# Chaining the last block's division and projection into the issue order of an attention + GLU kernel, with retuned scheduler constants and a VectorE-only prologue scaling

## Chip, cores, metric

The kernel runs on 1 core of a Trainium2 chip. The metric is the device time of one execution in microseconds (us); lower is better. Three runs of the kernel before gave a median of 854.28 us.

Engine names as in the profile: PE (TensorE, matmuls), PEld (its weight loads), DVE (VectorE), ACT (ScalarE), POOL (GpSimd), SP (SyncE, which issues most DMAs). PV is the product of probabilities and values. In the views a q behind a name (SPq) means that engine's sequencer, which waits and issues; "issue" is time in which the profile shows no wait. The granted clock (PEclk) is the share of its full clock that TensorE is given: 1.00 is full, 0.50 half. In code cuts `...` marks what is left out, and comments behind # are partly added here.

## The reference

Sequence 2048, width 640, 32 heads of 20, GLU width 1728, bf16:

```python
xn = layernorm(x)
s  = softmax(q k^T * 20**-0.5) v @ wo          # q, k, v = xn @ wqkv, 32 heads
g  = silu((sigmoid(xn @ w_gate) * (xn @ w_up)) @ w_down)
return x + s * g
```

## The kernel before

The kernel has three stages. In the *prologue* the rows of x (16 tiles of 128) are normalised, scaled, transposed, and the first keys and queries are made. In the *middle* 32 blocks of attention (8 groups of 4 heads, 4 query chunks of 512) run with the GLU woven in. In the *tail* comes what is left of the output projection, and the last block.

The instruction order of the middle is made when the program is built: a small Python loop keeps a model time for PE, ScalarE and VectorE and decides at each step what an engine gets next. Its decisions depend on a line of tuning constants:

```python
URGENT, ROUNDS, HOLD, SLACK, LEAD, LAG, D_LAST, D_LAST_END = 0.05, 3, 0.2, 0.6, 40.0, 0.0, 24, 16
D_ORD, M_ORD, WAIT3, FALL, M_END = 0, 1, 0.0, 1, 1.5
```

The result is a static order: each engine works its list from front to back, and a late item holds up all behind it.

Exponentials are shared. ScalarE does most of the 2048 score tiles with its exp, two per instruction (1024 columns), sometimes with a third of 512 columns. VectorE does the others by integer arithmetic (`iv`, then three passes over four tiles).

The prologue's scaling, some of it on GpSimd:

```python
POOL_XN = (0, 1, 4, 5)
...
(nc.gpsimd if eng == "POOL" else nc.vector).tensor_scalar(
    out=xns[k], in0=xts[k], scalar1=mvs[c][:, i, 0:1], scalar2=rstds[c][:, i, :],
    op0=ALU.subtract, op1=ALU.mult)
```

An output half-tile (128 rows, 320 columns) is an item of the issue order; there are 24 for the first three chunks. Its rows of x and of the gate `gq` come by DMA into one of three slots, and the result is stored from that slot:

```python
o2 = xfl[:, tt % 3 * KD * QC: ...]                         # the slot of row tile tt
nc.sync.dma_start(out=out_tiles[tt][0], in_=x2[...])       # x: waits for the store of row tile tt - 3
nc.sync.dma_start(out=out_tiles[tt][1], in_=gq_dram[...])
...
nc.vector.scalar_tensor_tensor(out=tmp, in0=st["ps"][:, 0:HD], scalar=0.25, in1=gqr[:, sl], ...)
nc.gpsimd.tensor_tensor(out=xr[:, sl], in0=tmp, in1=xr[:, sl], op=ALU.add)   # needs x
```

After the loop `tail_steps()` emitted the last block's division and projection in one go: copy `oacc`, transpose, divide, transpose back, with the early matmuls (those that don't need the last block's result) of four 512-column groups ("mains") in between; then the late matmul of each main (the one that needs it); then a fifth group ("rest", 128 columns of each of four row tiles), then the evictions.

Of the kernel before, what the change touches and what calls it, by code (L numbers as in the profile page):

```python
# [10 lines left out]
FP32 = mybir.dt.float32  # L11
# [7 lines left out]
P = 128  # L19
# [11 lines left out]
URGENT, ROUNDS, HOLD, SLACK, LEAD, LAG, D_LAST, D_LAST_END = 0.05, 3, 0.2, 0.6, 40.0, 0.0, 24, 16  # L31
D_ORD, M_ORD, WAIT3, FALL, M_END = 0, 1, 0.0, 1, 1.5
# [17 lines left out]
def kernel(  # L50
# [146 lines left out]
    ACT_STATS = (3, 6, 7, 11, 14, 15)  # L197
    POOL_XN = (0, 1, 4, 5)
    with tc.tile_pool(name="ln", bufs=2) as lp, \
# [68 lines left out]
        def s_xn(eng, k):  # L268
            c, i = divmod(k, 4)
            xns[k] = lp.tile([P, D], BF16, tag="xn", bufs=TT, name="xn")  # L270
            (nc.gpsimd if eng == "POOL" else nc.vector).tensor_scalar(
                out=xns[k], in0=xts[k], scalar1=mvs[c][:, i, 0:1], scalar2=rstds[c][:, i, :],
                op0=ALU.subtract, op1=ALU.mult)
# [63 lines left out]
        for c in range(NQC):  # L337
            ks = range(4 * c, 4 * c + 4)
            st = [Step(s_stats, (k,), {"ACT": 1.62} if k in ACT_STATS else {"DVE": 0.83},
                       (table,) if k in ACT_STATS else (), 3.2 + 0.5 * k, late=0.5 * c) for k in ks]  # L340
            rs = Step(s_rstd, (c,), {"POOL": 1.3}, st, late=2.0 * c)
            for k in ks:
                xn = Step(s_xn, (k,), {"POOL": 0.85} if k in POOL_XN else {"DVE": 0.40}, (rs,), late=2.0 * c)
                tr = Step(s_tr, (k,), {"PE": 0.6}, (xn, idt), take="tp", late=2.0 * c)
                evs.append(Step(s_ev, (k,), {"DVE": 0.46, "ACT": 0.62}, (tr,), give="tp", late=2.0 * c))
            km = Step(s_k, (c,), {"PE": 1.1}, (spread, *evs[4 * c:]), take="pk", late=2.0 * c)
            kts.append(Step(s_kt, (c,), {"ACT": 0.58}, (km, ones), late=2.0 * c))
            kms.append(Step(s_kmax, (c,), {"DVE": 0.62}, (km, kts[-1]), give="pk", late=2.0 * c))
            for i in range(2 if c < NVP else 0):
                vm = Step(s_v, (c, i), {"PE": 0.9}, evs[4 * c:], take="pv", late=2.0 * c + 5.0)  # L350
                Step(s_vev, (c, i), {"ACT": 0.33}, (vm, consts), give="pv", late=2.0 * c + 5.0)
# [319 lines left out]
    def mk_down(c, t4, h, at):  # L671
# [15 lines left out]
        def ev():  # L687
            gqs = w2.tile([P, HD], FP32, tag="gqs", bufs=2, name="gqs")
# [57 lines left out]
    def mk_out(tt, h, at):  # L746
# [21 lines left out]
        def ev():  # L768
            xr, gqr = out_tiles[tt]
            sl = slice(h * HD, (h + 1) * HD)  # L770
            tmp = w2.tile([P, HD], FP32, tag="gqs", bufs=2, name="otmp")
            nc.vector.scalar_tensor_tensor(out=tmp, in0=st["ps"][:, 0:HD], scalar=0.25,
                                           in1=gqr[:, sl], op0=ALU.mult, op1=ALU.mult)
            nc.gpsimd.tensor_tensor(out=xr[:, sl], in0=tmp, in1=xr[:, sl], op=ALU.add)
# [190 lines left out]

    def tail_steps():
        c0 = (NQC - 1) * QC
        mains = [scA[1][:, 0, :], scA[1][:, 1, :], bank[0], bank[1]]

        def early(dst, t4, sl, stop):  # L970
            for kd in range(t_l + 1):
                rows = P if kd < t_l else o_l
                nc.tensor.matmul(dst, lhsT=oU[0:rows, kd, c0 + t4 * P:c0 + (t4 + 1) * P], rhs=wo[0:rows, kd, sl],
                                 start=(kd == 0), stop=stop and kd == t_l, skip_group_check=True)

        def late_mm(dst, t4, sl):
            nc.tensor.matmul(dst, lhsT=o7[:, t4 * P:(t4 + 1) * P], rhs=wo_l[:, sl], start=False, stop=True,
                             skip_group_check=True)

        on = w2.tile([P, QC], FP32, tag="on", bufs=2, name="on")  # L980
        nc.vector.tensor_copy(out=on, in_=oacc)
        early(mains[0], 0, slice(0, 512), False)
        early(mains[1], 1, slice(0, 512), False)
        tps = scA[0][:, 0, :]
        for i in range(4):
# [367 lines left out]
```

## Time and profile before

The stages, read off the timeline (first score matmul, end of the last PV matmul):

| stage | us | what limits it |
|---|---|---|
| prologue | 0 to 37.2 | a chain over all engines, POOL in it |
| middle | 37.2 to 818.1 (780.9) | ACT, PE and DVE together |
| tail | 818.1 to 849.5 (31.4) | PE, with a stop; ACT idle |

The windows view of before, one line per stage; after the stretch and its length come each engine's busy us with the number of instructions, then the granted TensorE clock, the DMA share and GB/s:

```profile
core 0: us, PE busy (x) PEld busy (x) DVE busy (x) ACT busy (x) POOL busy (x), PEclk, DMA share, GB/s
0.00:37.20 37.20, 16.64 (x146) 11.10 (x149) 22.89 (x58) 23.07 (x50) 23.27 (x36) 1.00 0.46 123
37.20:818.10 780.90, 752.86 (x6108) 253.92 (x6161) 741.84 (x1127) 771.26 (x928) 55.34 (x42) 1.00 0.25 69
818.10:849.50 31.40, 22.44 (x118) 10.25 (x119) 12.15 (x23) 0.00 (x0) 11.56 (x14) 0.83 0.36 113
```

In the middle ACT is busy 771 of 781 us, PE 753, DVE 742. In the tail the mean clock is 0.83. The 1.00 of the prologue is not all true: the clock record begins at 23.1 us only, and before that the five key matmuls of 512 columns took 2.34 us (at 20.84 us, below), the spacing of half clock.

The timeline of before, prologue (start, duration, engine, line, operation, out<-in):

```profile
9.04 5.00 POOL L271 TENSOR_SCALAR xn<-xt,mv,rstd 128x640 bf16<-128x640 bf16 x2
...
14.09 0.72 PE L278 MATMUL tp<-ident,xn 128*128 128x128 bf16 x5 [1.77 <-POOL xn L271]
...
17.60 5.17 POOL L271 TENSOR_SCALAR xn<-xt,mv,rstd 128x640 bf16<-128x640 bf16 x2
...
20.34 0.72 PE L278 MATMUL tp<-ident,xn 128*128 128x128 bf16 x5 [4.02 <-POOL xn L271]
...
20.84 2.34 PE L140 MATMUL psk<-xnT,wqk_85 128*128 128x512 bf16 x5
```

Two scalings on POOL take 5.0 and 5.2 us. The transposes at 14.09 and 20.34 wait for POOL (the bracket names it), and the first key matmul follows the second of these at 20.84.

The chain of waits of before, tail (start, duration, what): each line is what released the next.

```profile
822.74 4.33 DMA xnT<-in_A_x_dram
...
827.20 0.80 POOL xnT L774
...
828.02 0.50 DVE otmp L772
...
828.57 1.93 PE bk_511 L765 x6
830.50 1.83 PE bk_510 L765 x6
...
832.54 3.78 PE scA_508 L973 x9
```

A load of x takes 4.33 us to land. POOL's add waits for it, DVE waits for POOL, and PE for the bank that DVE empties. After that nine matmuls of 512 columns take 3.78 us, 0.42 each. The windows view of before around that stop:

```profile
825.30:828.70 3.40, 1.88 (x11) 0.80 (x10) 0.49 (x1) 0.00 (x0) 1.50 (x2) 0.99 0.77 244
828.70:832.10 3.40, 3.40 (x12) 1.23 (x11) 0.98 (x2) 0.00 (x0) 2.36 (x4) 0.50 0.48 152
832.10:835.50 3.40, 3.18 (x8) 0.99 (x8) 1.09 (x2) 0.00 (x0) 0.79 (x1) 0.50 0.13 49
835.50:839.00 3.50, 3.50 (x21) 1.51 (x18) 1.17 (x3) 0.00 (x0) 0.00 (x0) 1.00 0.00 0
```

From 828.7 to 835.5 the clock is 0.50.

### The profile page before, as it was taken

How to read it: one execution, taken by the hardware profiler on the slowest of the kernel's cores; microseconds unless marked ns; L12 is line 12 of the kernel's file. 1: busy time of each engine (PE TensorE's matmuls, PEld its weight loads, DVE VectorE, ACT ScalarE, POOL GpSimd, SP SyncE). 2: the span in 40 equal slices, each digit the busy share in tenths (PEclk: the TensorE clock that was granted, in tenths of full speed). 3: DMA queues.
4: the chain of work that ended last, by engine and by line, in shares of the span. 5: the costliest groups of instructions: out<-in, count | busy, mean ns of one | idle time of the engine just before them, and what ended most of it. 6: DMA issues, size and time to landing. Idle time of an engine off the chain costs nothing.

```text
span 849.5 us, 16987 instructions
## 1 busy us (share of the span) xinstructions
PE 791.9 (93%) x6369; PEld 275.3 (32%) x6424; DVE 776.9 (91%) x1208; ACT 794.3 (94%) x978; POOL 90.2 (11%) x92
## 2 busy tenths in 40 slices
PE   1899999999999999999999999999999999999996
PEld 1532322333333323333333222333333222233342
DVE  7589999999899998998999999999989989999964
ACT  6799999999999999999999999999999999999940
POOL 7300000000000000000000010000000000001242
PEclk9999999999999999999999999999999999999997
DMA  5531311123221233213122222220411331112551
GB/s 152 149 91 43 79 50 39 51 61 79 65 65 52 59 84 84 65 39 80 41 60 57 67 79 65 73 79 26 124 60 46 84 84 44 29 46 70 184 161 65
DMA packets 92979, 62.21 MB, mean 73 GB/s; under 512 B 34648, under 2 KB 86408, under 8 KB 92896
## 3 DMA queue, kind: packets, MB, share of 16 engines
q1 hardware_dynamic: 92608, 60.79, 25.8%
q8 instruction: 50, 0.82, 0.4%
q14 instruction: 33, 0.27, 0.1%
q10 hardware_dynamic: 288, 0.33, 0.1%
HBM read 46.24 MB, written 12.39 MB: 69 GB/s over the span
## 4 chain that ended last, share of the span: by engine, by line
PE 34%; ACT 28%; DVE 27%; issue 6%; DMA 2%; POOL 2%; SPq 1%; POOLq 0%; DVEq 0%; ACTq 0%
DVE iv L1168 11%; PE oacc L896 7%; PE scA_508 L859 5%; PE scA_507 L859 5%; DVE pb L950 4%; DVE pb L947 3%; PE bk_511 L641 3%; DVE pb L944 3%; PE bk_510 L641 2%; PE bk_509 L641 2%; PE bk_511 L504 1%; PE bk_511 L679 1%; PE bk_510 L679 1%; ACT tnh L80 1%; PE bk_510 L504 1%
## 5 line engine op out<-in xcount | busy, mean ns | idle before, releaser
L950 DVE TENSOR_TENSOR pb<-iv,pb 128x2048 bf16<-128x2048 bf16 x121 | 150.8, 1246 | 0.4
L1168 DVE TENSOR_SCALAR iv<-bk_509 128x512 int16<-128x512 f32 x168 | 114.2, 680 | 8.6 <-PE bk_509 L859 8.5
L1168 DVE TENSOR_SCALAR iv<-bk_510 128x512 int16<-128x512 f32 x168 | 114.4, 681 | 7.1 <-PE bk_510 L859 6.9
L926 POOL TENSOR_TENSOR on_bf<-on,rl 128x512 bf16<-128x512 f32 x30 | 43.2, 1440 | 693.3 <-DMA rl<-rd 342.6
L1168 DVE TENSOR_SCALAR iv<-bk_511 128x512 int16<-128x512 f32 x148 | 101.0, 682 | 9.4 <-PE bk_511 L859 9.0
L944 DVE TENSOR_SCALAR pb<-iv 128x2048 int16<-128x2048 int16 x121 | 88.3, 730 | 2.6
L947 DVE TENSOR_SCALAR pb<-iv 128x2048 int16<-128x2048 int16 x121 | 88.2, 729 | 0.0
L859 PEld LDWEIGHTS <-kT_81 32*128 32x128 bf16 x1024 | 40.4, 91 | 142.1 <-issue 137.7
L859 PEld LDWEIGHTS <-kT_82 32*128 32x128 bf16 x1024 | 44.2, 91 | 122.6 <-issue 112.1
L641 PE MATMUL bk_511<-xnT,wgu 128*128 128x512 bf16 x262 | 75.6, 382 | 2.7 <-DVE iv L1168 0.7
L896 PE MATMUL oacc<-pb,v_84 128*21 128x512 bf16 x498 | 74.1, 382 | 0.4 <-DVE pb L950 0.4
L896 PE MATMUL oacc<-pb,v_83 128*21 128x512 bf16 x470 | 73.3, 382 | 0.9 <-DVE pb L950 0.7
L641 PEld LDWEIGHTS <-wgu 128*128 128x128 bf16 x520 | 39.0, 97 | 68.5 <-issue 47.1
L679 PEld LDWEIGHTS <-hT 128*128 128x128 bf16 x448 | 35.8, 97 | 45.8 <-issue 36.0
L896 PEld LDWEIGHTS <-v_84 128*21 128x21 bf16 x1273 | 26.2, 90 | 47.3 <-issue 36.2
L896 PEld LDWEIGHTS <-v_83 128*21 128x21 bf16 x1259 | 25.9, 90 | 47.2 <-issue 37.5
L641 PE MATMUL bk_510<-xnT,wgu 128*128 128x512 bf16 x125 | 37.4, 382 | 2.1 <-DVE iv L1168 1.1
L679 PE MATMUL bk_509<-wd,hT 128*128 128x320 bf16 (+1 forms) x168 | 32.5, 302 | 0.5 <-DVE gqs L689 0.3
L679 PE MATMUL bk_511<-wd,hT 128*128 128x320 bf16 (+1 forms) x168 | 31.8, 302 | 0.3 <-DVE hT L661 0.2
L859 PE MATMUL scA_507<-q_94,kT_82 32*128 32x512 bf16 x134 | 27.1, 383 | 2.5 <-ACT pt_2836 L80 0.9
L859 PE MATMUL scA_507<-q_93,kT_81 32*128 32x512 bf16 x141 | 27.9, 383 | 1.5 <-DVE q_93 L177 0.8
L859 PE MATMUL scA_508<-q_93,kT_81 32*128 32x512 bf16 x140 | 27.9, 384 | 1.1 <-ACT pt_6542 L80 0.3
(1790 smaller groups left out, 2303.8 us busy)
## 6 DMA issues: line engine op xcount, KB each, us to landing
wgu<-in_B_w_gate_dram SPq DMA_DIRECT2D x24, 320.0 KB
wgu<-in_B_w_up_dram SPq DMA_DIRECT2D x24, 320.0 KB
rl<-rd SPq DMA_DIRECT2D x120, 64.0 KB
gq_dram<-gqs SPq DMA_DIRECT2D x32, 160.0 KB
xnT<-gq_dram SPq DMA_DIRECT2D x12, 320.0 KB
xt<-in_A_x_dram SPq DMA_DIRECT2D x16, 160.0 KB
wd<-in_B_w_down_dram SPq DMA_DIRECT2D x1, 2080.0 KB
oU<-on_bf SPq DMA_DIRECT2D x104, 20.0 KB
```

The costliest lines, as they stand in the source:

```text
L80: return nc.scalar.add_instruction(mybir.InstActivation(func=func, name=nc.get_next_instruction_name(), engine=ENG.Activation, ins=[nc.sca ...
L504: nc.tensor.matmul(st["ps"][0:UC, :], lhsT=wus[u][:, kd, i, :], rhs=xnT[:, c, kd, :], start=(kd == 0), stop=(kd == KD - 1))
L641: nc.tensor.matmul(st[key][0:fs, :], lhsT=w[:, i, kd, ko * P:ko * P + fs], rhs=xnT[:, c, kd, :], start=(kd == 0), stop=(kd == KD - 1))
L679: nc.tensor.matmul(st["ps"][:, 0:HD], lhsT=hT[0:fsz[kf], kf, t4 * P:(t4 + 1) * P], rhs=wd[0:fsz[kf], kf, h * HD:(h + 1) * HD], start=(kf = ...
L859: nc.tensor.matmul(dst, lhsT=kTs[(b // NQC) % 2][32 * j:32 * j + 32, kt * P:(kt + 1) * P], rhs=qts[b % 3][32 * j:32 * j + 32, :], start=Tr ...
L896: nc.tensor.matmul(oacc[32 * j:32 * j + DH + 1, :], lhsT=lhsT, rhs=u["src"], start=first, stop=last, tile_position=(0, 32 * j), skip_group ...
L926: nc.gpsimd.tensor_tensor(out=on_bf, in0=on, in1=rl, op=ALU.mult)
L944: nc.vector.tensor_scalar(out=pb[:, 0, :, :].bitcast(I16), in0=iv, scalar1=0x7F80, scalar2=1, op0=ALU.bitwise_and, op1=ALU.bitwise_or)
L947: nc.vector.tensor_scalar(out=pb[:, 1, :, :].bitcast(I16), in0=iv, scalar1=0x007F, scalar2=0x3F00, op0=ALU.bitwise_and, op1=ALU.bitwise_or)
L950: nc.vector.tensor_tensor(out=pb[:, 1, :, :], in0=iv.bitcast(BF16), in1=pb[:, 1, :, :], op=ALU.mult)
L1168: nc.vector.tensor_scalar(out=d["iv"][:, j, :], in0=bank[bk], scalar1=B_OFF, scalar2=0.0, op0=ALU.add, op1=ALU.max)
```

## The change

Its intent: the last block's division should be issued step by step between the output half-tiles that are left, so that PE and DVE don't wait for each other; the prologue's scalings leave POOL; and the constants are tuned again. The core of the diff:

```diff
-URGENT, ROUNDS, HOLD, SLACK, LEAD, LAG, D_LAST, D_LAST_END = 0.05, 3, 0.2, 0.6, 40.0, 0.0, 24, 16
-D_ORD, M_ORD, WAIT3, FALL, M_END = 0, 1, 0.0, 1, 1.5
+URGENT, ROUNDS, HOLD, SLACK, LEAD, LAG, D_LAST, D_LAST_END = 0.25, 4, 0.15, 0.2, 40.0, 0.0, 20, 8
+D_ORD, M_ORD, WAIT3, FALL, M_END = 1, 0, 0.4, 1, 1.5
...
-    ACT_STATS = (3, 6, 7, 11, 14, 15)
-    POOL_XN = (0, 1, 4, 5)
+    L_ST, L_CH = 6.0, 2.0                 # statistics of later chunks rank behind the chain of earlier ones
+    ACT_STATS = (3, 7, 9, 11, 13, 15)
...
-            (nc.gpsimd if eng == "POOL" else nc.vector).tensor_scalar(
+            nc.vector.tensor_scalar(
...
-            kms.append(Step(s_kmax, (c,), {"DVE": 0.62}, (km, kts[-1]), give="pk", late=2.0 * c))
+            kms.append(Step(s_kmax, (c,), {"DVE": 0.62}, (km,), give="pk", late=L_CH * c))
...
-            tmp = w2.tile([P, HD], FP32, tag="gqs", bufs=2, name="otmp")
+            tmp = w2.tile([P, HD], FP32, tag="gqs", bufs=3, name="otmp")
...
-            nc.gpsimd.tensor_tensor(out=xr[:, sl], in0=tmp, in1=xr[:, sl], op=ALU.add)
+            add = nc.vector if h == 1 and claimed[0] == NJOB * NBLK else nc.gpsimd
+            add.tensor_tensor(out=xr[:, sl], in0=tmp, in1=xr[:, sl], op=ALU.add)
...
+    chain = [("DVE", 0.60, e_on), ("PE", 1.52, e_tr), ("DVE", 0.75, e_scale), ("PE", 0.42, e_back), ("DVE", 0.45, e_o)]
+    fill = [... the early matmuls of the four mains, then of the rest ...]
     def tail_steps():
-        ... (division, early and late matmuls, as told above)
+        for _, _, f in fill:
+            f()
+        for t4 in range(4):
+            late_mm(rest[:, t4 * EX:(t4 + 1) * EX], t4, slice(512, D))
+        for t4 in range(4):
+            late_mm(mains[t4], t4, slice(0, 512))
...
+            if free["PE"] <= now and chain and chain[0][0] == "PE" and chain_at <= now:
+                _, dur, f = chain.pop(0)      # the same for DVE; fill is taken when nothing else is left
```

More of the change, by code (lines that the diff above doesn't have):

```diff
@@ L338 @@
             ks = range(4 * c, 4 * c + 4)
-            st = [Step(s_stats, (k,), {"ACT": 1.62} if k in ACT_STATS else {"DVE": 0.83},
-                       (table,) if k in ACT_STATS else (), 3.2 + 0.5 * k, late=0.5 * c) for k in ks]
-            rs = Step(s_rstd, (c,), {"POOL": 1.3}, st, late=2.0 * c)
+            st = [Step(s_stats, (k,), {"ACT": 1.92} if k in ACT_STATS else {"DVE": 0.98},
+                       (table,) if k in ACT_STATS else (), 3.2 + 0.5 * k, late=L_ST * c) for k in ks]
+            rs = Step(s_rstd, (c,), {"POOL": 1.3}, st, late=L_CH * c)
             for k in ks:
-                xn = Step(s_xn, (k,), {"POOL": 0.85} if k in POOL_XN else {"DVE": 0.40}, (rs,), late=2.0 * c)
-                tr = Step(s_tr, (k,), {"PE": 0.6}, (xn, idt), take="tp", late=2.0 * c)
-                evs.append(Step(s_ev, (k,), {"DVE": 0.46, "ACT": 0.62}, (tr,), give="tp", late=2.0 * c))
-            km = Step(s_k, (c,), {"PE": 1.1}, (spread, *evs[4 * c:]), take="pk", late=2.0 * c)
-            kts.append(Step(s_kt, (c,), {"ACT": 0.58}, (km, ones), late=2.0 * c))
-            kms.append(Step(s_kmax, (c,), {"DVE": 0.62}, (km, kts[-1]), give="pk", late=2.0 * c))
+                xn = Step(s_xn, (k,), {"DVE": 0.42}, (rs,), late=L_CH * c)
+                tr = Step(s_tr, (k,), {"PE": 0.6}, (xn, idt), take="tp", late=L_CH * c)
+                evs.append(Step(s_ev, (k,), {"DVE": 0.46, "ACT": 0.62}, (tr,), give="tp", late=L_CH * c))
+            km = Step(s_k, (c,), {"PE": 1.1}, (spread, *evs[4 * c:]), take="pk", late=L_CH * c)
+            kts.append(Step(s_kt, (c,), {"ACT": 0.58}, (km, ones), late=L_CH * c))
+            kms.append(Step(s_kmax, (c,), {"DVE": 0.62}, (km,), give="pk", late=L_CH * c))
             for i in range(2 if c < NVP else 0):
-                vm = Step(s_v, (c, i), {"PE": 0.9}, evs[4 * c:], take="pv", late=2.0 * c + 5.0)
-                Step(s_vev, (c, i), {"ACT": 0.33}, (vm, consts), give="pv", late=2.0 * c + 5.0)
+                vm = Step(s_v, (c, i), {"PE": 0.9}, evs[4 * c:], take="pv", late=L_CH * c + 5.0)
+                Step(s_vev, (c, i), {"ACT": 0.33}, (vm, consts), give="pv", late=L_CH * c + 5.0)
             if c == 0:
@@ L687, in ev @@
         def ev():
-            gqs = w2.tile([P, HD], FP32, tag="gqs", bufs=2, name="gqs")
+            gqs = w2.tile([P, HD], FP32, tag="gqs", bufs=3, name="gqs")
             nc.vector.scalar_tensor_tensor(out=gqs, in0=st["td"], scalar=1.0, in1=st["ps"][:, 0:HD],
@@ L964, in tail_load @@
             nc.sync.dma_start(out=tail[t4][1], in_=gq_dram[r, :])
-    def tail_steps():
-        c0 = (NQC - 1) * QC
-        mains = [scA[1][:, 0, :], scA[1][:, 1, :], bank[0], bank[1]]
-        def early(dst, t4, sl, stop):
-            for kd in range(t_l + 1):
-                rows = P if kd < t_l else o_l
-                nc.tensor.matmul(dst, lhsT=oU[0:rows, kd, c0 + t4 * P:c0 + (t4 + 1) * P], rhs=wo[0:rows, kd, sl],
-                                 start=(kd == 0), stop=stop and kd == t_l, skip_group_check=True)
-        def late_mm(dst, t4, sl):
-            nc.tensor.matmul(dst, lhsT=o7[:, t4 * P:(t4 + 1) * P], rhs=wo_l[:, sl], start=False, stop=True,
-                             skip_group_check=True)
-        on = w2.tile([P, QC], FP32, tag="on", bufs=2, name="on")
-        nc.vector.tensor_copy(out=on, in_=oacc)
-        early(mains[0], 0, slice(0, 512), False)
-        early(mains[1], 1, slice(0, 512), False)
-        tps = scA[0][:, 0, :]
-        for i in range(4):
-            nc.tensor.transpose(out=tps[:, i * P:(i + 1) * P], in_=on[:, i * P:(i + 1) * P], identity=ident_f)
-        onq = div_scale(tps)
-        early(mains[2], 2, slice(0, 512), False)
-        tp2 = psum.tile([P, 2 * QC], BF16, name="tp2", tag="oacc")
-        for i in range(4):
-            nc.tensor.transpose(out=tp2[0:GC, i * P:(i + 1) * P], in_=onq[:, i, :], identity=ident)
-        early(mains[3], 3, slice(0, 512), False)
-        o7 = w2.tile([GC, QC], BF16, tag="on_bf", bufs=2, name="o7")
-        nc.vector.tensor_copy(out=o7, in_=tp2[0:GC, 0:QC])
@@ new lines, with early, late_mm @@
+    c0 = (NQC - 1) * QC
+    mains = [scA[1][:, 0, :], scA[1][:, 1, :], bank[0], bank[1]]
+    rest = bank[2]
+    last = {}
+    def early(dst, t4, sl, kd, start=True):
+        rows = P if kd < t_l else o_l
+        nc.tensor.matmul(dst, lhsT=oU[0:rows, kd, c0 + t4 * P:c0 + (t4 + 1) * P], rhs=wo[0:rows, kd, sl],
+                         start=(start and kd == 0), stop=False, skip_group_check=True)
+    def late_mm(dst, t4, sl):
+        nc.tensor.matmul(dst, lhsT=last["o"][:, t4 * P:(t4 + 1) * P], rhs=wo_l[:, sl], start=False, stop=True,
+                         skip_group_check=True)
@@ new lines, in e_on, with e_tr, e_scale, e_back @@
+    def e_on():
+        last["on"] = w2.tile([P, QC], FP32, tag="on", bufs=2, name="on")
+        nc.vector.tensor_copy(out=last["on"], in_=oacc)
+    def e_tr():
+        for i in range(4):
+            nc.tensor.transpose(out=scA[0][:, 0, i * P:(i + 1) * P], in_=last["on"][:, i * P:(i + 1) * P],
+                                identity=ident_f)
+    def e_scale():
+        last["q"] = div_scale(scA[0][:, 0, :])
+    def e_back():
+        last["t"] = psum.tile([P, 2 * QC], BF16, name="tp2", tag="oacc")
+        for i in range(4):
+            nc.tensor.transpose(out=last["t"][0:GC, i * P:(i + 1) * P], in_=last["q"][:, i, :], identity=ident)
@@ new lines, in e_o @@
+    def e_o():
+        last["o"] = w2.tile([GC, QC], BF16, tag="rl", bufs=1, name="o7")
+        nc.vector.tensor_copy(out=last["o"], in_=last["t"][0:GC, 0:QC])
+    chain = [("DVE", 0.60, e_on), ("PE", 1.52, e_tr), ("DVE", 0.75, e_scale), ("PE", 0.42, e_back), ("DVE", 0.45, e_o)]
+    fill = [(t4 - 2, 0.2133, lambda t4=t4, kd=kd: early(mains[t4], t4, slice(0, 512), kd))
+            for t4 in range(4) for kd in range(t_l + 1)]
+    fill += [(2, 0.07, lambda t4=t4, kd=kd: early(rest[:, t4 * EX:(t4 + 1) * EX], t4, slice(512, D), kd, t4 == 0))
+             for t4 in range(4) for kd in range(t_l + 1)]
@@ L995, in tail_steps @@
+    def tail_steps():
+        for _, _, f in fill:
+            f()
+        for t4 in range(4):
+            late_mm(rest[:, t4 * EX:(t4 + 1) * EX], t4, slice(512, D))
         for t4 in range(4):
             late_mm(mains[t4], t4, slice(0, 512))
-        rest = bank[2]
-        for t4 in range(4):
-            dst = rest[:, t4 * EX:(t4 + 1) * EX]
-            early(dst, t4, slice(512, D), False)
-            late_mm(dst, t4, slice(512, D))
-        tmps = [hfl[:, t4 * 2 * D:t4 * 2 * D + 1024].bitcast(FP32) for t4 in range(4)]
@@ L1003, in tail_steps @@
-        for t4 in range(4):
-            xr, gqr = tail[t4]
-            nc.vector.scalar_tensor_tensor(out=tmps[t4], in0=mains[t4], scalar=0.25, in1=gqr[:, 0:512],
-                                           op0=ALU.mult, op1=ALU.mult)
-            if t4 < 2:
-                nc.gpsimd.tensor_tensor(out=xr[:, 0:512], in0=tmps[t4], in1=xr[:, 0:512], op=ALU.add)
+        tmps = [hfl[:, t4 * 2 * D:t4 * 2 * D + 1024].bitcast(FP32) for t4 in range(4)]
         xg = wfl[:, 0:12 * D].rearrange("p (t u) -> p t u", u=3 * D)
@@ L1017, in tail_steps @@
                                 in1=xg[:, :, 512:D], op=ALU.add)
-        for t4 in (2, 3):
+        for t4 in range(4):
             xr, gqr = tail[t4]
-            nc.vector.tensor_tensor(out=xr[:, 0:512], in0=tmps[t4], in1=xr[:, 0:512], op=ALU.add)
+            nc.vector.scalar_tensor_tensor(out=tmps[t4], in0=mains[t4], scalar=0.25, in1=gqr[:, 0:512],
+                                           op0=ALU.mult, op1=ALU.mult)
+            add = nc.vector if t4 == 3 else nc.gpsimd
+            add.tensor_tensor(out=xr[:, 0:512], in0=tmps[t4], in1=xr[:, 0:512], op=ALU.add)
         for t4 in range(4):
@@ L1060, in due, with can_fill @@
             return total * min(1.0, progress() / (NBLK - M_END))
+        def can_fill(f):
+            if claimed[0] < NJOB * NBLK or cur is not None:
+                return False
+            if f < 0:
+                return slots[1]["a"] is None and slots[1]["ends"] <= now
+            return not items and all(it.bank != f for it in active if it.i < len(it.ops)) and flex[f] <= now
         def finish(item, t):
@@ L1078 @@
         guard = 0
-        while pv_block[0] < NBLK or items or glu_items or any(it.i < len(it.ops) for it in active):
+        chain_at = 1e9
+        while chain or items or glu_items or any(it.i < len(it.ops) for it in active):
             guard += 1
@@ L1114 @@
                 if free[eng] > now:
+                    continue
+                if chain and chain[0][0] == eng and chain_at <= now:
+                    _, dur, f = chain.pop(0)
+                    f()
+                    free[eng] = now + dur
+                    chain_at = now + dur + EL
                     continue
@@ L1198 @@
                 dcur = None
+            if free["PE"] <= now and chain and chain[0][0] == "PE" and chain_at <= now:
+                _, dur, f = chain.pop(0)
+                f()
+                free["PE"] = now + dur
+                chain_at = now + dur + PL
+                mode = "M"
             if free["PE"] <= now:
@@ L1308 @@
                         cur = None
+                elif nxt is None and fill and can_fill(fill[0][0]):
+                    free["PE"] = now + fill[0][1] + (T_MODE if mode != "M" else 0.0)
+                    fill.pop(0)[2]()
+                    mode = "M"
                 elif nxt == "PV":
@@ L1318 @@
                         pv_block[0] += 1
+                        if b == NBLK - 1:
+                            chain_at = now + dur + PL
             now += STEP
```

## The prediction

> **What bounds the kernel.** The timeline of before has three stages in its 849.5 us span: a prologue until the first score matmul at 37.2 us; the attention with the GLU woven in, until the last PV matmul at 818.1 us (781 us); and a tail of 31.4 us. In the middle stage three engines are saturated together (windows of 100 us: ScalarE 98-99%, VectorE 91-99%, PE 96-98%); ScalarE, whose waits list is almost empty, is nearest to its limit. In the tail ScalarE is idle.
>
> **What changes.** The diff adds a chain for the last division, but it also re-tunes the scheduler's constants, so the issue order of every engine changes. I counted both orders.
>
> 1. Prologue. Four xn scalings leave GpSimd, where two take 5.0 to 5.2 us (2.5 each), for VectorE, where they take 0.44 to 0.72 us. They hold up chunk 0: its transposes wait for GpSimd until 14.1 us, and again at 20.3 us for chunk 1 (timeline; this transpose stands ahead of the first K matmul, which starts at 20.8). GpSimd's rstd of chunk 3 waits behind them until 24.2 us. Following after's order with these durations: chunk 0 transposed about 14 us, first K matmul about 14, last scaling about 25.5, last K matmul about 28, first score 32.3 us (31 to 34). Gain about 5 us. VectorE gains 4 x 0.5 us; the kmax still waits for ScalarE, so nothing is won by dropping that dependency.
>
> 2. Middle. VectorE's exp jobs fall from 484 to 471 (13 x 0.68 us, and about 3.3 groups of passes at 2.7 us: some 17 us off). ScalarE gets 13 more and more triples: 139 instead of 102 of 512 columns (about 0.49 us start to start), 719 instead of 731 of 1024 (0.91 us): about +7 us. PE: ten fewer fills, 36 more mode changes (about 0.1 us each, e.g. 0.32 us for a fill of 0.21), 3 to 4 output tiles moved in from the tail: about +3 us. ScalarE's +7 us fits only if its hidden gaps shrink, which the more urgent fills intend. I take the stage as unchanged to slightly longer, +0.5 us (-4 to +5).
>
> 3. Tail. Before has 11 output half-tiles after the last PV, after about 7.5. Before's chain of waits shows 4.3 us for a load of x behind stores and gq loads, GpSimd adds of 0.8 us, and a PE idle gap near 827; from there matmuls run at half clock: nine of 512 columns take 3.78 us (0.42 each, against 0.21). TensorE: Matmul & The Clock Gate (the Trainium skill, Part 1) says that an idle window halves the clock; the windows view agrees (0.73 in 830-840). After: the division's chain hides among the output tiles, PE stays fed: 7.5 tiles x 1.03 us, transposes 1, 20 fills x 0.21, 20 small 2.2, late 0.9: last matmul about 16 us after the last PV. Then VectorE 0.7+0.7+4x0.6, a GpSimd add 1.1 behind two others, store 3.5: tail about 25 us. Gain about 6.5.
>
> **Sum.** 854.3 - 5 + 0.5 - 6.5 = 843.3 us.
>
> **Right if:** first score near 32 us; last PV near 813.5; tail near 25 with granted clock over 0.9 and no GpSimd xn; last matmul before the final VectorE evictions with 0.21 us spacing.
>
> **Wrong if:** the re-tuned middle gains or loses more than 5 us (most likely source of error: ScalarE bound by its extra triples, or less starving); the x loads of tiles 10 and 11 land late and VectorE, in order, stalls on its new adds, so that PE halts on banks and its clock halves again; VectorE's scalings collide with GpSimd's memsets.
>
> Chances: faster by over 2% 0.13, within 2% 0.86, slower 0.01. Range 836.5 to 850 us.

## The result

After runs in 842.92 us (median of 4, 841.47 to 843.3); before, with one more run beside it, in 853.94 us. The ratio is 0.988, 95% interval 0.984 to 0.9919. Here and below a ratio is the mean time of one kernel's runs over that of the other's of the same rounds, so it is not quite the ratio of the medians quoted.

The windows view of after, by stage:

```profile
core 0: us, PE busy (x) PEld busy (x) DVE busy (x) ACT busy (x) POOL busy (x), PEclk, DMA share, GB/s
0.00:33.00 33.00, 17.77 (x148) 11.44 (x153) 23.63 (x62) 23.02 (x50) 13.37 (x32) 1.00 0.51 139
33.00:814.50 781.50, 753.97 (x6112) 259.37 (x6166) 729.43 (x1109) 772.97 (x953) 56.58 (x45) 1.00 0.25 70
814.50:839.80 25.30, 16.61 (x102) 7.68 (x100) 12.38 (x24) 0.00 (x0) 7.55 (x7) 0.90 0.32 105
```

The prologue is 4.2 us shorter, the middle 0.6 us longer (781.5), the tail 6.1 us shorter (25.3). The prediction had -5, +0.5 and -6.5. The profiled runs took 851.22 us (before, below its median) and 841.47 us (after).

The timeline of after, prologue:

```profile
9.18 1.93 DVE L271 TENSOR_SCALAR xn<-xt,mv,rstd 128x640 bf16<-128x640 bf16 x4
...
12.30 2.45 DVE L271 TENSOR_SCALAR xn<-xt,mv,rstd 128x640 bf16<-128x640 bf16 x4
...
14.52 2.29 PE L140 MATMUL psk<-xnT,wqk 128*128 128x512 bf16 x5 [1.01 <-ACT xnT L281]
...
23.71 1.51 DVE L271 TENSOR_SCALAR xn<-xt,mv,rstd 128x640 bf16<-128x640 bf16 x4
...
32.98 0.39 PE L860 MATMUL scA<-q,kT 32*128 32x512 bf16 x2 [0.79 <-DVE q L177]
```

The first four scalings now take 1.93 us on DVE, the first key matmul starts at 14.52, and the first score matmul at 32.98.

The chain of waits of after, tail:

```profile
814.51 1.02 PE bk L765 x6
...
817.84 5.13 PE bk L765 x30
...
823.03 2.42 PE scA L976 x9
825.45 4.53 PE bk L976 x30
829.98 0.34 PE bk L980 x4
...
830.34 0.70 DVE hT L1020
...
831.07 0.70 DVE wd L1025
...
831.87 1.90 DVE hT L1029 x3
833.76 1.14 POOL wd L1032
```

No DMA and no POOL stands in it until the last matmul; from 814.5 to 830.3 it is PE alone. 8.6 us follow the end of the last matmul (831.2). The windows view of after in the tail shows a clock of 1.00:

```profile
820.00:825.00 5.00, 4.94 (x26) 1.99 (x24) 2.47 (x6) 0.00 (x0) 1.18 (x2) 1.00 0.43 142
825.00:830.00 5.00, 5.00 (x34) 2.26 (x34) 0.32 (x1) 0.00 (x0) 0.97 (x1) 1.00 0.09 33
```

The page's shares of the chain that ended last, over the whole span. Before:

```profile
PE 34%; ACT 28%; DVE 27%; issue 6%; DMA 2%; POOL 2%; SPq 1%; POOLq 0%; DVEq 0%; ACTq 0%
```

After:

```profile
ACT 49%; PE 28%; DVE 13%; issue 6%; DMA 2%; SPq 1%; POOL 0%; POOLq 0%; ACTq 0%; DVEq 0%
```

ScalarE's share of the chain grew from 28% to 49%, while the middle kept its length.

So the stage times are as predicted. But the change has three parts that can be taken apart, and the stage times don't tell which of them earned the tail.

### The profile page after: what moved, and what is told of

Same layout as the page of the kernel before. It is cut to its first block, busy times and chain, and to the rows that moved or that the text cites. A ratio compares the mean times of both kernels' runs of the same rounds, so it can differ in the third digit from the quotient of the medians.

```text
span 839.8 us, 16932 instructions
## 1 busy us (share of the span) xinstructions
PE 788.4 (94%) x6354; PEld 278.5 (33%) x6411; DVE 765.4 (91%) x1194; ACT 796.0 (95%) x1003; POOL 77.5 (9%) x84
## 4 chain that ended last, share of the span: by engine, by line
ACT 49%; PE 28%; DVE 13%; issue 6%; DMA 2%; SPq 1%; POOL 0%; POOLq 0%; ACTq 0%; DVEq 0%
ACT pt L80 44%; PE scA L860 8%; PE oacc L897 5%; DVE iv L1194 5%; PE bk L679 4%; PE bk L641 3%; ACT tnh L80 3%; DVE pb L951 2%; PE bk L765 2%; PE bk L504 2%; DVE pb L945 1%; DVE pb L948 1%; DMA ld<-on 1%; PE psk L140 1%; ACT td L80 1%
## 5 line engine op out<-in xcount | busy, mean ns | idle before, releaser
L80 ACT ACTIVATE pt<-scA 128x1024 bf16<-128x1024 f32 (+1 forms) x729 | 720.2, 1153 | 4.6 <-PE bk L860 2.9
L1194 DVE TENSOR_SCALAR iv<-bk 128x512 int16<-128x512 f32 x471 | 318.6, 682 | 31.7 <-PE bk L860 30.2
L860 PE MATMUL scA<-q,kT 32*128 32x512 bf16 x1448 | 282.6, 382 | 16.7 <-ACT pt L80 9.6
L860 PE MATMUL bk<-q,kT 32*128 32x512 bf16 x600 | 215.5, 383 | 2.0 <-DVE iv L1194 1.7
L897 PE MATMUL oacc<-pt,v 128*21 128x512 bf16 x1577 | 183.1, 382 | 0.6 <-ACT pt L80 0.3
L860 PEld LDWEIGHTS <-kT 32*128 32x128 bf16 x2048 | 88.7, 91 | 261.6 <-issue 246.8
L897 PE MATMUL oacc<-pb,v 128*21 128x512 bf16 x942 | 152.9, 382 | 1.8 <-DVE on L910 1.5
L641 PE MATMUL bk<-xnT,wgu 128*128 128x512 bf16 x471 | 142.6, 383 | 3.6 <-issue 1.7
L80 ACT ACTIVATE pt<-bk 128x512 bf16<-128x512 f32 x129 | 94.5, 733 | 4.0 <-PE bk L860 3.8
L679 PE MATMUL bk<-wd,hT 128*128 128x320 bf16 x448 | 86.9, 302 | 1.2 <-DVE iv L1194 0.7
```

What stands on the lines that cost most here:

```text
L80: return nc.scalar.add_instruction(mybir.InstActivation(func=func, name=nc.get_next_instruction_name(), engine=ENG.Activation, ins=[nc.sca ...
L641: nc.tensor.matmul(st[key][0:fs, :], lhsT=w[:, i, kd, ko * P:ko * P + fs], rhs=xnT[:, c, kd, :], start=(kd == 0), stop=(kd == KD - 1))
L679: nc.tensor.matmul(st["ps"][:, 0:HD], lhsT=hT[0:fsz[kf], kf, t4 * P:(t4 + 1) * P], rhs=wd[0:fsz[kf], kf, h * HD:(h + 1) * HD], start=(kf = ...
L860: nc.tensor.matmul(dst, lhsT=kTs[(b // NQC) % 2][32 * j:32 * j + 32, kt * P:(kt + 1) * P], rhs=qts[b % 3][32 * j:32 * j + 32, :], start=Tr ...
L897: nc.tensor.matmul(oacc[32 * j:32 * j + DH + 1, :], lhsT=lhsT, rhs=u["src"], start=first, stop=last, tile_position=(0, 32 * j), skip_group ...
L1194: nc.vector.tensor_scalar(out=d["iv"][:, j, :], in0=bank[bk], scalar1=B_OFF, scalar2=0.0, op0=ALU.add, op1=ALU.max)
```

## The experiments

Twelve kernels ran, in three groups, each kernel on one chip with the kernel before. Stage times come from the profiled execution of each; "left" is the number of 320-column matmuls behind the last PV in the issue order; "block 1" is the time from the first score to the first copy of the accumulator, "start clock" is explained below the table.

| kernel | median us | ratio, interval | first score | middle | tail | left | block 1 | start clock |
|---|---|---|---|---|---|---|---|---|
| before | 853.94 | 1 | 37.2 | 780.9 | 31.4 | 63 | 28.7 | full |
| after | 842.92 | 0.988 (0.984 to 0.9919) | 33.0 | 781.5 | 25.3 | 44 | 28.2 | full |
| prologue only | 850.15 | 0.9954 (0.9926 to 0.9983) | 33.0 | 783.3 | 32.6 | 63 | 31.8 | half |
| tail only | 853.28 | 0.9984 (0.9948 to 1.002) | 37.4 | 782.7 | 32.9 | 63 | 30.0 | half |
| constants only | 846.2 | 0.9908 (0.9873 to 0.9943) | 37.8 | 784.4 | 23.0 | 44 | 30.0 | half |
| scalings only | 850.67 | 0.9961 (0.9929 to 0.9992) | 33.9 | 780.5 | 32.2 | 63 | 28.7 | full |
| after, old tail | 841.9 | 0.9859 (0.9822 to 0.9896) | 32.1 | 783.8 | 23.6 | 44 | 30.0 | half |
| after, late matmuls per group | 838.68 | 0.9826 (0.979 to 0.9863) | 33.1 | 782.2 | 22.0 | 44 | 28.1 | full |
| before, gap filled | 851.23 | 0.9981 (0.9935 to 1.0027) | 37.3 | 781.9 | 30.0 | 63 | 30.0 | half |
| one constant only | 844.51 | 0.9906 (0.9874 to 0.9938) | 37.2 | 784.7 | 20.6 | 28 | 30.0 | half |
| after, start filled | 841.09 | 0.9854 (0.9818 to 0.989) | 32.9 | 781.7 | 25.2 | 44 | 28.2 | full |
| best | 837.0 | 0.9815 (0.9786 to 0.9844) | 32.6 | 779.4 | 22.0 | 44 | 28.2 | full |
| after, more ScalarE | 847.8 | 0.9938 (0.9909 to 0.9967) | 32.7 | 788.3 | 25.2 | 44 | 29.5 | half |
| after, more PE | 844.33 | 0.9901 (0.9868 to 0.9934) | 32.8 | 787.8 | 25.3 | 44 | 30.3 | half |

"Start clock: half" means that the windows view granted less than 1.00 in the first 12 us after the first score matmul of that profiled run. In the six runs without it block 1 took 28.1 to 28.7 us, in the eight with it 29.5 to 31.8.

### Prologue only

```diff
 # the kernel before, with the prologue of after: its ACT_STATS, L_ST, L_CH, scalings on VectorE, kmax without kts[-1]
```

> The kernel before with after's prologue alone (all scalings on VectorE, other statistics on ScalarE, other lateness); the rest of the issue order is untouched. Theory: the start of the attention is worth its full 4.2 us, because all that follows is one static order: first score matmul at 33.0 us (37.2 before), middle 781 us and tail 31.4 us as before, time 4.2 us less, ratio 0.995. Rival: the weight loads behind the prologue or the GLU's first tiles wait longer, and the earlier start is given back in the first 100 us: ratio above 0.998.

Measured: first score at 33.03 us, ratio 0.9954. The time came as expected, but not along the expected path in the profiled run: it lost 3.1 us again in block 1 (31.8 against 28.7). The windows view of this kernel just after its first score:

```profile
35.00:40.00 5.00, 5.00 (x34) 2.94 (x32) 1.53 (x4) 3.58 (x5) 0.00 (x0) 0.50 1.07 362
```

and of after:

```profile
35.00:40.00 5.00, 4.46 (x49) 2.61 (x48) 3.79 (x7) 5.00 (x8) 0.00 (x0) 1.00 1.07 362
```

So the loss there is PE at half clock and not a late weight load. The table above shows that this befalls kernels with the old and the new prologue alike. It differs between runs of the same instructions: the kernel "more PE" below has after's order until its first added matmul at 55.8 us, and had the half clock where after had not. The times of before scatter too, though only the mean clock of each run is known: in the second group seven runs of the kernel before took from 849.69 us at a mean clock of 0.997 to 857.37 us at 0.983, with the others in between (849.69, 851.08, 851.27, 853.74, 853.79, 855.57, 857.37 at 0.997, 0.995, 0.994, 0.989, 0.994, 0.989, 0.983). So I take it for scatter between runs, not for an effect of the change. Comparing the middles of two profiled runs to a microsecond needs this first.

### Scalings only

```diff
-    POOL_XN = (0, 1, 4, 5)
+    POOL_XN = ()
```

> The kernel before with the four scalings moved from GpSimd to VectorE and nothing else of the prologue's change. Theory: the scalings on GpSimd (2.5 us each) are the prologue's hold-up, so this alone wins most of the 4.2 us: first score matmul at 33 to 35 us, ratio 0.995 to 0.9975. Rival: the order of the statistics (chunk 0's scalings ahead of the later chunks' statistics) is what wins; then the first score stays above 36 us, ratio above 0.998.

Measured: first score at 33.92 us, ratio 0.9961. Of the 4.2 us, 3.3 come from taking four scalings off POOL; the new order of the statistics adds 0.9, which is little more than scatter: with one and the same prologue the first scores in the table differ by up to 1 us. The theory holds.

### Tail only

```diff
 # the kernel before, with chain, fill, the new tail_steps, VectorE adds and gqs bufs=3; old constants, old prologue
```

> The kernel before with the division's chain in the issue order, the new last steps and the VectorE adds, but the old constants and prologue. Its issue order up to the last PV matmul is that of before, so 11 output half-tiles are left after it (63 matmuls of 320 columns, 44 in after). Theory: the tail falls from 31.4 us to 25.3 + 3.4 x 1.03 = about 28.8 us (PE kept at full clock), time 2.6 us less, ratio 0.997; the clock granted in the tail is over 0.95 until the last matmul. Rival: the tail's new order is worth all of the 6.1 us by which after's tail is shorter: ratio 0.993.

Both were wrong. The tail did not shrink at all (32.9 us), and the ratio of 0.9984 is within the noise of 1. By the time alone the theory's 0.997 would still be possible; the trace refutes it. The chain of waits of this kernel in the tail:

```profile
822.43 3.37 DMA out_dram<-xnT
...
825.81 4.13 DMA xnT<-in_A_x_dram
...
830.44 0.49 DVE otmp L772
```

and its windows view just after that:

```profile
830.00:835.00 5.00, 3.81 (x12) 1.47 (x13) 2.47 (x6) 0.00 (x0) 2.59 (x3) 0.60 0.48 143
```

With the old constants 63 matmuls are left, and PE still stops for a late x (4.13 us, behind a store of 3.37), and then runs at 0.60 of the clock. Hiding the division among the output tiles doesn't help where the stop comes from their loads.

### Constants only

```diff
-URGENT, ... = 0.05, 3, 0.2, 0.6, 40.0, 0.0, 24, 16
-D_ORD, M_ORD, WAIT3, FALL, M_END = 0, 1, 0.0, 1, 1.5
+URGENT, ... = 0.25, 4, 0.15, 0.2, 40.0, 0.0, 20, 8
+D_ORD, M_ORD, WAIT3, FALL, M_END = 1, 0, 0.4, 1, 1.5
```

> The kernel before with after's ten scheduler constants and nothing else. Theory: the middle stage is worth nothing by itself (781 us, as 780.9 and 781.5 in before and after), but it now holds 3 to 4 output half-tiles more, so the old tail starts with 7.5 instead of 11 of them and is about 3 us shorter, if it still stalls once: time 3 us less, ratio 0.9965. Rival 1: the extra 7 us of ScalarE work cost time in the middle: ratio 1.003 or more. Rival 2: the constants win in the middle, beyond the moved tiles: ratio below 0.993.

Measured: ratio 0.9908, about 7.8 us, more than twice of what the theory gave. Of the constants in these two lines nine differ. Rival 2 had a ratio below 0.993, but for another reason: the middle is no shorter. The old tail, with 44 matmuls left, takes 23.0 us, and it does not stall:

```profile
825.00:830.00 5.00, 4.94 (x30) 2.36 (x29) 1.80 (x4) 0.00 (x0) 2.07 (x4) 1.00 0.74 208
830.00:835.00 5.00, 4.94 (x25) 2.04 (x25) 2.70 (x6) 0.00 (x0) 2.77 (x4) 1.00 0.25 88
```

My theory had kept the stop; in fact it is gone, and with it the half clock. The middle (784.4) contains a start at half clock that cost about 1.3 us of block 1, so it is 2 us or so longer than before's.

### After with the old tail

```diff
 # the kernel before, with the constants and the prologue of after; tail_steps and adds as before
```

> After without its tail: the kernel before with after's constants and after's prologue. In the constants-only run the old tail took 23.0 us from the last PV matmul, against 25.3 in after with the same 44 matmuls of 320 columns left; the last matmul came 16.7 us after the last PV in both, but then 6.3 us against 8.6 followed. Theory: the new tail contributes nothing, its last steps even cost 2.3 us, as all evictions now wait for the late matmuls: ratio 0.9855 against before (after: 0.988). Rival (the prediction): the chain among the output tiles keeps PE fed and earns the gain; then this kernel is 2 us or more slower than after, ratio 0.9905.

Measured: 0.9859, tail 23.6 us. The theory holds in direction: without the new tail code the kernel is not slower than after (0.988); the difference of the two ratios itself is within their intervals. In the traces the old end is shorter by about 2 us after the last matmul: 6.3 us (833.3 to 839.5) against 8.6. PE stopped once here, for 0.71 us at 826.0: the copy of the accumulator stood on VectorE behind evictions that waited, through POOL, for a late x. The clock stayed at 1.00. The prediction's account of the tail falls with this run and the two before it.

### One constant only

```diff
-D_ORD, M_ORD, WAIT3, FALL, M_END = 0, 1, 0.0, 1, 1.5
+D_ORD, M_ORD, WAIT3, FALL, M_END = 0, 0, 0.0, 1, 1.5
```

> The kernel before with one constant changed (the order in which a projection looks for a free bank). By its issue order 28 matmuls of 320 columns are left after the last PV (63 in before, 44 in after), with ScalarE's work almost as in before (102 to 110 exps of 512 columns, 731 to 728 of 1024: +1 us). It separates the moved tiles from ScalarE's extra work. Theory: the middle takes the 35 moved matmuls (4.9 us of PE) without becoming longer, as in after, and the tail, old steps and all, has neither gap nor half clock: 23 us less 16 x 0.14, about 20.5 us; about 9 us less in all, ratio 0.989 to 0.991. Rival: PE time moved into the middle costs what it takes there, and only the gap and the clock (5 to 6 us) are won: middle 786 us, ratio 0.993 to 0.995.

Measured: 0.9906 with a tail of 20.6 us, both as expected. One constant that leaves fewer tiles behind gives as much as all nine. The middle is 784.7 us; less some 1.3 us of a half-clock start it is about 2.5 us longer than before's, for 4.9 us of matmuls moved in. So the moved tiles are about half free there, not wholly. Why this constant leaves fewer tiles I did not pursue.

### Before with the gap filled

```diff
         def mm(kd):
+            if kd == 0 and tt == TT - 5 and h == 0:
+                for _ in range(6):
+                    nc.tensor.matmul(scA[0][:, 1, :], lhsT=ident, rhs=oU[:, 0, 0:QC], start=True, stop=True,
+                                     skip_group_check=True)
```

> The kernel before with six more matmuls of 512 columns (1.3 us, result unused, into a free bank) put where PE idles for 1.5 us in the tail, ahead of the last output row tile's first half. The idle time itself and the late loads stay. Theory: it is the half clock after the gap (0.50 for 5 us, nine matmuls of 512 columns at 0.42 us) that lengthens before's tail: with PE busy in the gap the clock stays at 1.00 and the tail shortens by 3 to 4 us, ratio 0.9955 to 0.9965. Rival: the loads of x set the tail's end and the clock is a symptom: tail unchanged, ratio above 0.998.

Measured: ratio 0.9981, tail 30.0 us: in time inconclusive. The trace explains it. Its windows view shows that the clock stays full:

```profile
825.00:830.00 5.00, 3.91 (x20) 1.69 (x20) 0.89 (x2) 0.00 (x0) 0.00 (x0) 1.00 0.80 239
830.00:835.00 5.00, 3.63 (x19) 1.57 (x19) 2.56 (x5) 0.00 (x0) 4.56 (x6) 1.00 0.32 105
```

and its chain of waits that the load of x landed later in this run:

```profile
823.80 6.07 DMA xnT<-in_A_x_dram
...
830.00 0.80 POOL xnT L778
```

PE still stood idle for 1.89 us after the six matmuls (829.48 to 831.37), longer than the 1.52 us in before, and kept its clock; the closing list tells what decides.

In the four kernels with 63 matmuls left and the old tail the load is issued 4.6 us after the last PV. It took 4.33 us in before, 5.13 in scalings only, 5.61 in prologue only, and their tails of 31.4, 32.2 and 32.6 us are each 27.0 to 27.1 us longer than it. With the gap filled the load took 6.07 us and the tail is 24.0 us longer than it. So the half clock was worth 3.1 us by this estimate, as the theory says, and the late load that sets the length of the stop took 1.7 us of it back. The load is the cause, the clock is a surcharge on it.

### After, late matmuls per group

```diff
-        for _, _, f in fill:
-            f()
-        for t4 in range(4):
-            late_mm(rest[:, t4 * EX:(t4 + 1) * EX], t4, slice(512, D))
-        for t4 in range(4):
-            late_mm(mains[t4], t4, slice(0, 512))
+        for grp in (0, 1, "rest", 2, 3):
+            # the early matmuls of this group, then its late one (or four)
...
+        # evictions in the same order: mains 0 and 1, the rest, mains 2 and 3
```

> After with each of the five last groups finished (its late matmul) directly after its own early matmuls, in the order main 0, main 1, rest, main 2, main 3, and evicted in that order. The number of matmuls and their total time are unchanged. Theory: VectorE and GpSimd evict four groups while PE still works; after the last matmul only one eviction (0.6), one VectorE add (0.7) and the store (3.4) remain: 4.7 to 5.2 us in place of 8.6, tail 21.3 to 22 us, ratio 0.984. Rival: mode changes and bank waits on PE eat it, or the stores are bound by the add of the rest: tail above 24 us, ratio above 0.987.

Measured: ratio 0.9826, tail 22.0 us (25.3 in after). The timeline of this kernel at its end:

```profile
826.77 1.29 DVE L1028 SCALAR_TENSOR_TENSOR hT<-scA,wd 128x512 f32<-128x512 f32 x2 [0.32 <-PE scA L980]
...
829.84 0.69 DVE L1033 SCALAR_TENSOR_TENSOR hT<-bk,wd 128x512 f32<-128x512 f32 x1 [1.78 <-POOL wd L1031]
...
831.37 1.29 DVE L1028 SCALAR_TENSOR_TENSOR hT<-bk,wd 128x512 f32<-128x512 f32 x2
...
831.54 0.39 PE L980 MATMUL bk<-wo_l,o 80*128 80x512 bf16 x1
...
832.69 1.15 DVE L1031 TENSOR_TENSOR wd<-hT,wd 128x512 bf16<-128x512 f32 x1
```

VectorE evicts mains 0 and 1 from 826.77 on and the rest at 829.84, while PE works on until 831.9; 5.3 us follow the last matmul instead of 8.6. The last value of the division was there early in after too (its copy ended at 818.6, the last matmul at 831.2), so nothing had forced the late matmuls to the end.

### After, start filled

```diff
         def s_bound(eng):
-            q_bound(pq[0], 0, pq[1])
+            warm = psP.tile([P, 512], FP32, tag="pv", bufs=2, name="warm")
+            for i in range(8):
+                if i == 5:
+                    q_bound(pq[0], 0, pq[1])
+                nc.tensor.matmul(warm, lhsT=ident, rhs=xnT[:, 0, 0, :], start=True, stop=True, skip_group_check=True)
```

> After with eight more matmuls of 512 columns (result unused) in the two gaps of 1.3 and 0.8 us which PE has around the bound's matmul, before the first score matmul. Three of the five profiles of my runs had the clock at 0.50 for some 5 us from there on, and their first block took 1.3 to 3.1 us longer (30.0 to 31.8 against 28.2 to 28.7); the profiled runs of before and after had not. Theory: whether PE is slowed there differs from run to run, and this makes the scatter of the times; with the gaps filled it never is: the four times lie within 1.5 us and the median is 0.5 to 1.5 us below after's, ratio 0.9865. Rival: the scatter has another source: same median, same scatter; or the first score is delayed by the added work: ratio 0.989 or more.

Measured: ratio 0.9854, four times between 840.1 and 843.14. The profile shows the clock at 1.00 through block 1 (28.2 us), but after's profiled run had that too, the scatter of 3 us is twice what I expected, and the interval holds after's ratio. By itself this run decides nothing.

### Best

```diff
 # late matmuls per group, start filled, and for the last key chunk:
+                kms.append(Step(s_kmax, (c,), {"DVE": 0.62}, (km,), late=L_CH * c))
+                kts.append(Step(s_kt, (c,), {"ACT": 0.58}, (km, ones, kms[-1]), give="pk", late=L_CH * c))
```

> The per-tile late matmuls, the matmuls that fill PE's gaps before the first score, and for the last key chunk the maximum ahead of the key copy (they read one bank in turn, and VectorE waited 2.07 us for ScalarE there, of which the copy is 0.7). Theory: the tail stays 21.9 us, the first score comes 0.7 us earlier (32.3 us), the clock is at 1.00 from there: 0.7 to 1.5 us below the per-tile kernel, ratio 0.981 to 0.982. Rival: the maximum is not on the path, and the clock fills add nothing: ratio 0.9826 or more.

Measured: 837.0 us, ratio 0.9815, six runs within 2.3 us (835.75 to 838.06), where eleven runs of before beside it spread from 848.68 to 857.0. The last maximum starts at 29.81 us, against 30.57 in after. The first score came at 32.6 us, 0.4 earlier than with the late matmuls alone, but the seven kernels with after's order of these steps had it between 32.1 and 33.1, so a gain there is not shown. This is the fastest version, correct like all the others; its interval overlaps that of the per-group kernel, so only the latter's part is sure.

### After, more ScalarE

```diff
+                            if nexp % 45 == 20:
+                                junk = w2.tile([P, QC], BF16, tag="junk", bufs=1, name="junk")
+                                exp_act(junk, scA[nexp % 2][:, 0, :])
```

> After with sixteen more exps of 512 columns on ScalarE (result unused), spread evenly over the middle: 16 x 0.49 = 7.8 us of ScalarE. It measures what ScalarE's time is worth in the middle, where the retuned constants had added 7 us of it and the stage did not lengthen. Theory of the prediction (ScalarE nearest to its limit): in a static order nearly all of it shows, middle 787 to 789.5 us, ratio near 0.996. Rival: the middle has hidden gaps on ScalarE that soak it up, and PE is the limit: middle below 785 us, ratio below 0.992.

Measured: ratio 0.9938, about 5 us over after, for 7.8 us of ScalarE; middle 788.3 us, 1.3 of it a half-clock start. From the end of block 1 to the last accumulator copy it took 759.0 us, against 753.6 in after: 5.4. The page's chain shares of this kernel:

```profile
ACT 55%; PE 24%; DVE 11%; issue 7%; DMA 2%; SPq 0%; POOLq 0%; POOL 0%; ACTq 0%; DVEq 0%
```

Six to seven tenths of added ScalarE time show. That is nearer to the theory than to the rival; the interval of the ratio is wide enough to hold the rival's 0.992 as well, and the trace decides.

### After, more PE

```diff
+                        if jobs and nfill % 45 == 20:
+                            for _ in range(2):
+                                nc.tensor.matmul(scA[nfill % 2][:, 0, :], lhsT=ident, rhs=wo[:, 0, 0:QC], start=True,
+                                                 stop=True, skip_group_check=True)
```

> After with 32 more matmuls of 512 columns on PE (into a bank that is overwritten next), two ahead of every 45th fill: 32 x 0.213 = 6.8 us of PE, spread evenly over the middle. Companion of the ScalarE run. Theory (ScalarE nearest to the limit): less than half shows, middle below 785 us, ratio below 0.9925. Rival (PE is the limit, or the static order passes on any delay): 5 us or more, middle over 786 us, ratio 0.994 or more.

Measured: ratio 0.9901, about 1.8 us over after, for 6.8 us of PE. By the times the theory holds, though the interval holds after's 0.988 too. The profiled run, the slowest of the six (847.61 us), had a half-clock start of 2.1 us and passed on 4.2 us beyond block 1, which looks like the rival. But its clock was at 0.50 a second time, from 796.2 to 803.0 us. At the 31st of the 32 accumulator copies (796.6 us) it was only 2.0 us behind after, counted from the end of block 1, where the ScalarE kernel was 5.4 behind; the rest came with that stretch. Between the two kernels, on one chip, the medians are 3.5 us apart. So ScalarE's time costs more than PE's, of which about three tenths show.

## Why the prediction was right

**The total and the stages.** Predicted 843.3 us, measured 842.92. First score 32.3 predicted, 33.0 measured; last PV 813.5 and 814.5; tail 25 and 25.3; last matmul 16 us after the last PV, measured 16.7. That the sum met the median to 0.4 us is partly luck: the stages of the two profiled runs differ by 9.7 us (849.5 to 839.8), the medians by 11.0 and the prediction by 11.0, because before's profiled run was one of its faster ones.

**Prologue: right, for the reason given.** The scalings on POOL were the hold-up: moving them alone gives 3.3 of the 4.2 us. The expected scatter of VectorE's scalings was there: the second four took 2.45 us where the first took 1.93, with POOL's memsets beside them. "Nothing is won by dropping that dependency" fits after's trace, where VectorE still waits 1.79 and 2.07 us for ScalarE's copy of the keys before the last two maxima; no run tests it alone.

**Middle: right in size, and the gaps shrank as it asked.** The retuned constants give ScalarE 139 exps of 512 columns in place of 102 and 719 in place of 731 of 1024, which is 7 us more at the spacings that the prediction read from before (0.49 and 0.91 us). The stage did not lengthen, and ScalarE's busy time in it rose by 1.7 us only (771.26 to 772.97). The ScalarE run says that this is not because ScalarE had room: 7.8 us more cost about 5. The packed traces show what gave way. From the start of one exp to the next start on ScalarE the median is 0.90 us (1024 columns) and 0.48 (512) in both kernels. What the stage's exps take beyond these medians, in sum, fell from 28.4 us in before to 20.9 in after. These are the hidden gaps of the prediction; busy time doesn't show them, as the records of neighbouring exps overlap. The sum is 19.5 to 23.5 us in the runs with the retuned constants (27.2 in the PE run), and 27.9 to 30.6 in those without them, the one-constant run (29.5) among these. So it is another constant, or several, that does it; which is open.

**Tail: right in size, wrong in its account.** The step that failed reads "the division's chain hides among the output tiles, PE stays fed". PE stays fed, but not because of the chain, and the constants are what removed the stop. The new tail alone leaves the stop where it was (tail 32.9 us, ratio 0.9984); the constants alone remove it (tail 23.0 us, 0.9908); after with the old tail is not slower than after (0.9859). What fits all traces is that the number of output tiles left decides, though no run changes that number alone. PE needs 2.06 us for a row tile (two half-tiles at 1.03), while each needs loads into one of three slots which wait for a store, and these took 4.1 to 6.1 us to land. With 63 matmuls left the late x is in the chain in all five kernels that have them; with 44 or 28 the clock stayed full up to the last matmul of the tail in all nine, and PE stopped in one of them only (0.71 us, after with the old tail). The prediction had the count (11 half-tiles against 7.5) and used it for PE's work only. Its sum came out because it took the tail with the new constants as one piece. The warning about VectorE's in-order adds came true and was harmless: they waited 0.67 and 0.97 us for x, while PE had the fills.

**What the prediction missed.** The new order of the late matmuls costs 2 us and more: no eviction starts before 830.3 us, and the last matmul ends at 831.2. And the start of the middle has a state of its own, full or half clock; half cost 1.3 to 3.1 us in the first block.

Open: what else varies in the middle (the same order took 753.6 us in after and 751.5 in the best kernel from block 1's end to the last copy, both at full clock), and how near to three tenths the value of PE's time there is.

## What to carry to other kernels

When a change mixes new code with retuned constants, run the constants alone: here they earned about two thirds of the gain, most likely because they leave fewer load-bound tiles for the stage in which nothing covers their loads, and the new tail code earned nothing that showed. A PE stop of 1.5 us can cost three more afterwards through the clock, so look at the granted clock behind each gap, and first remove the wait, then fill what is left of it. Put the last dependent matmul of each group right behind the group, so that evictions run beside the remaining matmuls: that gave more than the whole new chain.

## What the Trainium skill lacked or had wrong

- "TensorE: Matmul & The Clock Gate", Part 1 and the section on HAM oscillation: the half clock is told to follow at least one idle window of some 3.4 us, and the rule given is to have no PE-idle gaps above that. (A second failure mode there has short, frequent idle times, without a length.) Here no gap was that long; the longest after the clock had first come up was 2.76 us. In before a window of 3.4 us in which PE was busy for 1.88 us (one gap of 1.52 us) was followed by two such windows at 0.50 (828.7 to 835.5). In each of the fourteen traces the clock changes only at whole multiples of 3.413 us from its first change, which comes at 13.6 to 26.0 us. In the stretches of that grid just ahead of the 14 drops (those before the last matmul) PE was busy for 0.66 to 2.39 us; the least busy stretch without a drop behind it had 1.74. So what counts is how the idle time falls into these stretches. With six matmuls put into the gap the clock stayed at 1.00: what was left of it fell into two stretches with 2.40 and 2.54 us busy. The page's state times of about 3.4 us and the spacing of a cold 512-column matmul (about 427 ns; 0.42 us here) agree with this.
- The same page, on run-to-run variation: it puts the warm-up ramp at under 1% of a typical span and calls the window free-running; it does not say that a later drop varies in the same way. Here the clock was full from 13.6 to 26.0 us on, and in eight of fourteen profiled runs it fell again at 32.8 to 39.7 us, which cost 1.3 to 3.1 us in the first block; runs of one kernel spread from 849.69 to 857.37 us with the mean clock (0.997 to 0.983). That is under 1%, but as large as the effects under study.
- "GPSIMD Engine Reference", section 4.1: elementwise work with one input is called roughly line-rate on GpSimd next to VectorE. The scaling of 128x640 bf16 with two per-partition scalars took 2.50 us at the least on GpSimd and 0.43 us (median) on VectorE in before. For two inputs (about 2x slower by the page) the add of 128x320 took 0.79 against 0.49 us, 1.6x.
- No page that I looked up gives the time to landing of a whole load beside other traffic: a load of 160 KB took 4.13 to 6.07 us to land in the tail, at a DMA share of about 0.8, and this set the length of before's tail.
